# New places for two gatings' steps in expert 0, a last expert of 384 + 256 rows, and a second network in six tiles of three blocks

## The chip, the cores and the metric

The kernel runs on one core of a Trainium2 chip. The time is that of one execution on the device in microseconds (us), and less is better. The core's engines each work through a queue of their own: TensorE (PE, matmuls), VectorE (DVE), ScalarE (ACT), GpSimd (POOL, which also issues the indirect DMAs) and SyncE (SP, which issues most plain DMAs). A wait in a queue holds up everything behind it in that queue.

## The reference

Attention over windows of 64 positions, a mixture of eight experts with the two best for each token, and a dense second network. In short:

```
scores = q @ k.T / 8, masked to 0 <= i - j < 64;  x = softmax(scores) @ v      # 4 x 8 heads x 576 x 64
x = heads put side by side                                                     # 2304 tokens x 512
noisy = x @ w_gate + log1p(exp(x @ w_noise)) * noise                           # 8 experts
top2 = the two best experts of each token, with softmax weights
x = sum over the two: weight * (relu(x @ w1[e]) @ w2[e])                        # 512 -> 1024 -> 512
h = x @ w_in;  out = (h * clip(h + 3, 0, 6) / 6) @ w_out                       # 512 -> 2048 -> 512
```

All data are float32. The tokens are 18 blocks of 128.

## The kernel before, in words

Every product of the two networks is made from a high and a low part of each operand with three matmuls (high x high, high x low, low x high). A half is called `xh`/`xl` for tokens, `hh`/`hl` for the hidden layer, and `h..`/`l..` with two more letters for a weight.

**Attention** runs first, about 137 us. PE's order is written by hand; the order on DVE, ACT and POOL is made by a scheduler. Its last step for a group of heads, `normalise`, writes `xbuf` on DVE and so frees the PSUM tile `pv`.

**Gating** (`gate_batch`) works in four batches of 4, 5, 4 and 5 blocks. For each it makes the noisy logits (`logits`, `logits_back`, `s1` to `s2`), takes the two best (`s3`, `s3b`, which ends in the mask `mk`), counts the places on PE (`s4`), and derives a token's position (`s5`). `place` then builds for each block and choice two matrices on DVE, `pa` and `pbt`, whose product on PE adds token numbers into `px`; `total` adds this to `iacc`. After the last batch `iacc` becomes `idx`, the table by which `gather` fetches tokens from `x_rows`. Of the third batch only the start, and of the fourth nothing, is done during attention. The rest is hung into expert 0's first sub-stage by two lists of numbers, `when_late` (third) and `when` (fourth): number i below 32 is the place after the matmuls of step d = i % 4 of hidden block f = i // 4, and above that a place in the second layer. From expert 0 on, the order of all queues is the order of the program.

**Experts.** An expert handles up to 640 rows (5 blocks, m = 0 to 4) in two sub-stages: expert 0 in 256 + 384 rows (`SUBS`), the others in 320 + 320. A sub-stage (`expert_sub`) first makes the hidden layer, eight blocks f of 12 matmuls, each followed by `hh` on ACT and `hl` on DVE; then, for each m, 24 matmuls of the second layer, a copy `y` and its store to `y_rows`. The PSUM tiles of f are `ph` (three buffers), and every fourth one is `ph4` (one buffer), so f = 3 and f = 7 share it. Other work is hung into a sub-stage by `put(function, key)`, with keys ("f", f, 0 or 1), ("d", f, d), ("m", m, 0 to 3) and ("s", m, f).

**The second network** takes the blocks in tiles, 2, 3, 3, 3, 3, 2 and 2 blocks (`TILES`). A tile has two halves; each makes eight hidden blocks of 12 matmuls over the whole tile, then 24 matmuls per block. Its input is made by `fetch(t, i)` (8 indirect DMAs on POOL per block i of tile t, four pieces for each of a token's two experts, into `xg`), `combine` (ACT scales, DVE adds) and `tokens` (DVE transposes into `xt`, ACT makes `xh`, DVE `xl`). A fetch of token block n reads the rows of the first min(5, n + 1) blocks m of all experts, so block 0 needs m = 0 of expert 7 stored:

```
tt = BASES[t] + i
left = ybuf[0:E * 128 * min(CAP, tt + 1)]
```

Tile 0's two blocks are fetched, combined and turned during expert 7's second sub-stage; later tiles' during the tile before.

Of the kernel before, what the change touches and what calls it, by code (L numbers as in the profile page):

```python
# [32 lines left out]

HOLD = SUBS[0][1] * 128
# [11 lines left out]
def attention_moe_kernel(ctx, tc, q, k, v, w_gate, w_noise, noise, w1, w2, w_in, w_out, out):  # L46
# [282 lines left out]

    def gate_batch(ts, bank):  # L330
# [4 lines left out]
        def tmp(nm, shape=(E,), dt=F32):  # L335
            T[nm] = gp.tile([128, 5, *shape], dt, name=nm)[:, :n]
            return T[nm]
# [87 lines left out]

        def place(i, j):
            def run():
                t = t0 + i
                a = gp.tile([128, 128], F16, name="pa", bufs=4)
                bt = gp.tile([128, E * NT], F16, name="pbt", bufs=4)  # L430
                dve.tensor_scalar(a, iota128, T["qf"][:, i, j:j + 1], None, op0=OP.is_equal)
                dve.tensor_scalar(bt, iotab, T["cf"][:, i, j:j + 1], tokid[:, t:t + 1],
                                   op0=OP.is_equal, op1=OP.mult)
                PL[t, j] = (a, bt)
# [6 lines left out]
            return run, mm  # L441
# [24 lines left out]

        def runs(i):
            for run, mm in pl[2 * i:2 * i + 2]:
                run()

        def mms(i):
            for run, mm in pl[2 * i:2 * i + 2]:
                mm()
# [6 lines left out]
        if t0 + n == NT:  # L480
            chain = firsts + [logits, logits_back, s1, s1b, s2, s3, s3b, s4, s5]
            return (chain + [lambda i=i: runs(i) for i in range(n)] + [lambda i=i: mms(i) for i in range(n)] +
                    [total, weigh, piece_rows])
# [174 lines left out]
    fill, late, coming = [], [], []  # L658
# [9 lines left out]
    with tc.manual_schedule(engines={mybir.EngineType.PE}):  # L668
# [10 lines left out]
        for g in range(NG + 2):  # L679
            n, j = divmod(g, 3)  # L680
            for past in ((g - 3, g - 2) if g > 2 and g % 2 else ()):
# [3 lines left out]
                if p == HP - 1 and jj == 2 and b < B - 1:  # L685
                    t = gate_batch(DONE[b], lambda: gps.tile([128, 512], F32, name="g"))
                    if b == B - 2:
                        cut = [f for _, f in t].index(None) + 5
                        t, late = t[:cut], [f for _, f in t[cut:] if f]
# [190 lines left out]
    def expert_sub(e, s, at):  # L880

        m0, m1 = SUBS[s]


        if e == 0:
# [4 lines left out]
        if e == 0 or s == 0:  # L890
            HH[:] = [[ep.tile([128, 384], F32R, name=f"{nm}{f}") for f in range(8)] for nm in ("hh", "hl")]
# [52 lines left out]
    TILES = (2, 3, 3, 3, 3, 2, 2)  # L944
# [29 lines left out]
    for e in range(E):  # L974
# [7 lines left out]
        if e == 0:  # L982
            t = gate_batch(DONE[B - 1], lambda: eps.tile([128, 512], F32, name="py", bufs=2))
            t += [lambda m=m: gather(0, m) for m in range(A1, M)] + [lambda m=m: build(0, m) for m in range(A1, M)]
# [4 lines left out]
            assert len(when) == len(t) and len(when_late) == len(late)  # L989
            for i, f in list(zip(when_late, late)) + list(zip(when, t)):  # L990
                put(f, *(("d", i // 4, i % 4) if i < 32 else ("s", (i - 32) // 8, (i - 32) % 8)))
# [14 lines left out]
        if 0 < e < 5:  # L1006
            for f in range(8):
                put(lambda: next(table, None), "f", f, 1)
        expert_sub(e, 0, at)
# [31 lines left out]
        else:  # L1041
# [120 lines left out]
    for t, ni in enumerate(TILES):  # L1162
# [10 lines left out]
        if t + 1 < len(TILES):  # L1173
# [11 lines left out]
            if 0 < t < len(TILES) - 2:  # L1185
                put(lambda: fetch(t + 2, 0), 1, 1, 3)
# [7 lines left out]
        for half in range(2):  # L1194
# [18 lines left out]
            for i in range(ni):  # L1213
# [51 lines left out]
```

## Time and profile before

| | |
|---|---|
| median of 3 runs | 1007.03 us (1004.6 to 1007.49) |
| the profiled execution | 1009.37 us, of which its span 1007.6 |
| busy share of the span | PE 98%, DVE 57%, ACT 46%, POOL 32% |
| mean granted clock of PE | 0.991 |
| chain that ended last | PE 80%, DVE 9%, DMA 5%, ACT 3% of the span |

The profile is of one execution. Times in it count from the start of its span; what lies outside the span (1.8 us) is not in it. The chain follows the last instruction back, each time to what released it or to what stood ahead of it on its engine.

### The profile page before, as it was taken

The numbers are of one execution on the slowest core, as the hardware profiler recorded it, in microseconds if no ns is written. First come the engines' busy times: TensorE is split into PE (matmuls) and PEld (weight loads), VectorE is DVE, ScalarE is ACT, GpSimd is POOL, SyncE is SP. The second block draws the span as 40 slices with busy tenths as digits, with TensorE's granted clock in tenths as the row PEclk, the third lists the DMA queues.
The fourth block names the chain that finished last, engine by engine and source line by source line (L and its number), as shares of the span: only waits on it lengthen the run. The fifth ranks groups of instructions, "written<-read, shape, count | busy, mean of one in ns | idle before, by whom it ended". The sixth has DMA issues, their size and how long they took to land.

```text
span 1007.6 us, 17479 instructions
## 1 busy us (share of the span) xinstructions
PE 983.8 (98%) x6392; PEld 893.7 (89%) x6392; DVE 573.9 (57%) x1550; ACT 467.8 (46%) x1032; POOL 324.7 (32%) x351
## 2 busy tenths in 40 slices
PE   8989898999999999999999999999999999999998
PEld 7979886999897999999998988989988998899997
DVE  6687975556777776666667656444333433344322
ACT  6867651444544454444454546434333433334333
POOL 2122202732535334242431276732343234410000
PEclk9999998999999999999999999999999999999999
DMA  9897441546656666656666454200111002000000
GB/s 168 169 221 190 119 147 50 165 139 201 214 163 197 192 184 193 186 186 209 215 195 196 151 191 133 70 23 19 58 32 46 24 26 63 27 27 22 11 11 23
DMA packets 116395, 122.43 MB, mean 122 GB/s; under 512 B 69840, under 2 KB 78288, under 8 KB 116304
## 3 DMA queue, kind: packets, MB, share of 16 engines
q1 hardware_dynamic: 96144, 86.17, 31.0%
q0 software_dynamic: 9488, 19.94, 7.1%
q10 hardware_dynamic: 10672, 15.15, 4.1%
q8 instruction: 51, 0.84, 0.3%
q14 instruction: 40, 0.33, 0.1%
HBM read 92.91 MB, written 28.31 MB: 120 GB/s over the span
## 4 chain that ended last, share of the span: by engine, by line
PE 80%; DVE 9%; DMA 5%; ACT 3%; issue 2%; POOL 0%; ACTq 0%; DVEq 0%; SPq 0%
PE ph L1204 6%; PE ph L1202 6%; PE ph L1203 6%; PE ph L903 6%; PE ph L904 6%; PE ph L905 6%; PE py L1225 5%; PE py L1224 5%; PE py L1223 5%; PE py L923 4%; PE py L924 4%; PE py L925 4%; PE s L242 3%; PE pv L295 2%; PE tr L1225 1%
## 5 line engine op out<-in xcount | busy, mean ns | idle before, releaser
L522 POOL DMA_INDIRECT xg<-x_rows,idx x140 | 145.1, 1037 | 221.2 <-DVE xt L533 169.8
L959 POOL DMA_INDIRECT xg<-y_rows,rows x144 | 144.3, 1002 | 222.4 <-DVE xg L967 74.5
L1207 DVE SCALAR_TENSOR_TENSOR g<-g,ph 128x384 f32<-128x384 f32 (+1 forms) x112 | 55.7, 497 | 158.8 <-ACT g L1206 154.5
L1206 ACT ACTIVATE g<-ph,three 128x384 f32<-128x384 f32 (+1 forms) x112 | 60.0, 536 | 100.7 <-PE ph L1204 97.7
L911 DVE SCALAR_TENSOR_TENSOR hl<-ph,hh 128x320 fp32r<-128x320 f32 (+2 forms) x128 | 61.0, 487 | 74.1 <-ACT hh L910 74.1
L1212 DVE TENSOR_TENSOR hl<-g,hh 128x384 fp32r<-128x384 f32 (+1 forms) x112 | 56.2, 502 | 58.9 <-ACT hh L1210 56.1
L910 ACT ACTIVATE hh<-ph 128x320 fp32r<-128x320 f32 (+2 forms) x128 | 54.6, 436 | 65.2 <-PE ph L905 61.2
L1210 ACT CAST hh<-g 128x384 fp32r<-128x384 f32 (+1 forms) x112 | 52.4, 467 | 63.8 <-DVE g L1207 63.8
L527 ACT CAST xh<-xt 128x512 fp32r<-128x512 f32 (+1 forms) x60 | 33.6, 570 | 81.9 <-DVE xt L533 81.2
L528 DVE TENSOR_TENSOR xl<-xt,xh 128x512 fp32r<-128x512 f32 (+1 forms) x60 | 37.2, 630 | 39.7 <-ACT xh L527 39.7
L242 PE MATMUL s<-kt,qbd 128*128 128x128 f32 x288 | 43.7, 293 | 0.2 <-ACT kt L227 0.2
L242 PEld LDWEIGHTS s<-kt,qbd 128*128 128x128 f32 x288 | 40.2, 207 | 0.6 <-ACT kt L227 0.5
L157 POOL TENSOR_SCALAR vt<-vt 64x520 f32<-64x520 f32 (+1 forms) x32 | 19.3, 604 | 57.0 <-DMA vt<-in_v_dram 53.2
L533 DVE STREAM_TRANSPOSE xt<-xg 128x512 f32<-128x512 f32 x53 | 37.4, 706 | 0.4
L762 DVE SCALAR_TENSOR_TENSOR na<-mag,raw 128x256 f32<-128x256 f32 x64 | 26.9, 420 | 12.7 <-DMA w_out<-na 5.1
L759 ACT ACTIVATE mag<-raw 128x256 f32<-128x256 f32 x64 | 27.6, 431 | 12.6 <-DVE na L768 12.6
L257 ACT ACTIVATE pb<-sm,mx 128x128 f32<-128x128 f32 x90 | 30.0, 397 | 5.8 <-DVE mx L250 5.7
L768 DVE CUSTOM_DVE_ANT_0 na<-mag,nr 128x512 uint16<-128x512 uint16 x64 | 27.3, 426 | 9.5 <-DVE mag L767 0.5
L931 ACT COPY y<-py 128x512 f32<-128x512 f32 x33 | 19.3, 584 | 27.1 <-PE py L925 14.1
L270 ACT COPY ptb<-pt 128x384 f32<-128x384 f32 x48 | 23.1, 480 | 12.7 <-PE pt L265 10.7
L767 DVE SCALAR_TENSOR_TENSOR mag<-na,mag 128x256 int32<-128x256 int32 x64 | 27.2, 425 | 2.2
L295 PE MATMUL pv<-vt,ptb 128*64 128x65 f32 x640 | 26.1, 226 | 1.8 <-DVE xbuf L314 1.8
(520 smaller groups left out, 3201.7 us busy)
## 6 DMA issues: line engine op xcount, KB each, us to landing
wraw<-in_moe_w_dram SPq DMA_DIRECT2D x60, 512.0 KB, 4.6
y_rows<-y ACTq DMA_DIRECT2D x40, 256.0 KB, 3.4
raw<-in_moe_w_in_dram SPq DMA_DIRECT2D x32, 256.0 KB, 3.8
raw<-in_moe_w_out_dram SPq DMA_DIRECT2D x32, 256.0 KB, 3.0
rq<-in_q_dram SPq DMA_DIRECT2D x32, 144.0 KB, 3.7
rk<-in_k_dram SPq DMA_DIRECT2D x32, 144.0 KB, 2.9
x_rows<-xbuf SPq DMA_DIRECT2D x18, 256.0 KB
out_dram<-y ACTq DMA_DIRECT2D x17, 256.0 KB, 2.2
```

Of the source, the lines that this page charges most:

```text
L242: pe.matmul(s[:, i, :], l, KT[n][:, k0:k0 + 128], start=(g in LIGHT), stop=(g in LIGHT or i == 2))
L522: pool.indirect_dma_start(out=t[:, i], out_offset=None, in_=pieces(xrows), in_offset=bass.IndirectOffsetOnAxis(ap=idx4[:, i, e, m:m + 1], ...
L903: pe.matmul(p, wh[:, fs], xh[:, d, :n], start=(d == 0), stop=False)
L904: pe.matmul(p, wh[:, fs], xl[:, d, :n], start=False, stop=False)
L905: pe.matmul(p, wl[:, fs], xh[:, d, :n], start=False, stop=(d == 3))
L911: dve.scalar_tensor_tensor(hl[f][:, cs], p, 0.0, hh[f].bitcast(F32)[:, cs], op0=OP.max, op1=OP.subtract)
L959: pool.indirect_dma_start(out=g[:, r], out_offset=None, in_=pieces(left), in_offset=bass.IndirectOffsetOnAxis(ap=rows4[:, r, tt, j:j + 1], ...
L1202: pe.matmul(p, wh[:, c], xh[:, d, :n], start=(d == 0), stop=False)
L1203: pe.matmul(p, wh[:, c], xl[:, d, :n], start=False, stop=False)
L1204: pe.matmul(p, wl[:, c], xh[:, d, :n], start=False, stop=(d == 3))
L1206: act.activation(g, p, AF.Relu, bias=three)
L1225: pe.matmul(py[i], gl[f][:, ms], wh[:, ws], start=False, stop=(f == NF - 1))
```

## The change

It has three parts.

1. In expert 0 the rest of the third batch (now from `logits_back` on) and the fourth batch are hung at new places by a table, `steps`, with the same numbers i as before. On DVE some of the two batches' steps are interleaved, one instruction of each in turn (`weave`); for that, `place` is cut in its two instructions. `pa` and `pbt` have eight buffers instead of four, and `gw`, `qf` and `cf` two instead of one.
2. Expert 7 is split 384 + 256 (`LAST`). The fetches of tile 0's three blocks begin in its first sub-stage, and two of the three combinations stand in the hidden layer of its second one.
3. The second network has six tiles of three blocks.

```diff
-            when = [0, 1, 3, 5, 7, 10, 12, 12, 13, 14, 16, 18, 28, 28, 30, 31, 31, 32, 33,
-                    36, 37, 38, 39, 40, 40, 41, 44, 40, 40, 40, 45, 46, 47]
-            when_late = [2, 3, 14, 14, 24, 24, 25, 26, 27, 30]
+            steps = {0: [a_back, turns[0], a_s1, turns[1]],
...
+                     10: [lambda: weave(a_5(), b_2())],
+                     12: [b_s3],
+                     16: [lambda: weave(b_3b(), a_parts(0))],
+                     20: [lambda: weave(a_parts(1))],
+                     23: [b_s4],
+                     24: [lambda: a_mms(0)],
+                     26: [lambda: a_mms(1), lambda: weave(b_5(), a_parts(2) + a_parts(3))],
+                     28: [lambda: weave(b_parts(0))],
+                     33: [lambda: a_mms(2), lambda: a_mms(3), lambda: weave(b_parts(1)), a_total],
+                     34: [lambda: b_mms(0), lambda: weave(b_parts(2))],
...
+                     38: [lambda: b_mms(4), b_total] + [lambda m=m: gather(0, m) for m in range(A1, M)],
...
+    def weave(*lists):
+        for fs in itertools.zip_longest(*lists):
+            for f in fs:
+                if f:
+                    f()
...
-                a = gp.tile([128, 128], F16, name="pa", bufs=4)
-                bt = gp.tile([128, E * NT], F16, name="pbt", bufs=4)
+                PL[t0 + i, j] = (gp.tile([128, 128], F16, name="pa", bufs=8),
+                                 gp.tile([128, E * NT], F16, name="pbt", bufs=8))
...
+LAST = ((0, 3), (3, CAP))
...
+        if e + 1 == E:
+            put(lambda: fetch(0, 0), "m", 1, 2)
+            put(lambda: fetch(0, 1), "m", 2, 2)
         expert_sub(e, 0, at)
...
-            for i in range(2):
-                put(lambda i=i: fetch(0, i), "f", 3 * i, 0)
-                put(lambda i=i: combine(0, i), "m", A1 + i, i)
-                put(lambda i=i: tokens(0, i), "m", A1 + i, 1 + i)
+            for i, (c, k) in enumerate(((("f", 0, 0), ("f", 1, 0)), (("f", 3, 0), ("f", 4, 0)),
+                                        (("m", 3, 1), ("m", 3, 2)))):
+                put(lambda i=i: combine(0, i), *c)
+                put(lambda i=i: tokens(0, i), *k)
+            put(lambda: fetch(0, 2), "f", 2, 0)
+            put(lambda: fetch(1, 0), "m", 4, 2)
...
-            put(lambda: fetch(1, 0), "m", A1 + 2, 0)
...
-    TILES = (2, 3, 3, 3, 3, 2, 2)
+    TILES = (3,) * 6
...
-            if 0 < t < len(TILES) - 2:
+            if t < len(TILES) - 2:
                 put(lambda: fetch(t + 2, 0), 1, 1, 3)
```

What this does to DVE's queue is shown at three places, each before and after. A row is line, operation, output and inputs, and size; a number behind a name tells tiles of one name apart.

First, DVE in attention, among the placements of a gating batch (about 72 us). Before:

```order
L310 RECIPROCAL rs_1354<-rs_1354 128x4
L250 ISA sm_1387,mx_1386<-s_1382,far_135 128x128
L250 ISA mx_1386 128x1
L250 ISA sm_1387,mx_1386<-s_1382,far_135 128x128
L250 ISA mx_1386 128x1
L250 ISA sm_1387,mx_1386<-s_1382,far_135 128x128
L250 ISA mx_1386 128x1
L431 TENSOR_SCALAR pa_1442<-iota128_127,qf_1285 128x128
L432 TENSOR_SCALAR pbt_1443<-iotab_129,cf_1286,tokid_131 128x144
L431 TENSOR_SCALAR pa_1446<-iota128_127,qf_1285 128x128
L432 TENSOR_SCALAR pbt_1447<-iotab_129,cf_1286,tokid_131 128x144
L314 TENSOR_TENSOR xbuf_191<-pv_1211,rs_1354 128x8x32
```

After:

```order
L445 TENSOR_SCALAR pa_1504<-iota128_127,qf_1283 128x128
L448 TENSOR_SCALAR pbt_1505<-iotab_129,cf_1284,tokid_131 128x144
L312 RECIPROCAL rs_1354<-rs_1354 128x4
L252 ISA sm_1387,mx_1386<-s_1382,far_135 128x128
L252 ISA mx_1386 128x1
L252 ISA sm_1387,mx_1386<-s_1382,far_135 128x128
L252 ISA mx_1386 128x1
L252 ISA sm_1387,mx_1386<-s_1382,far_135 128x128
L252 ISA mx_1386 128x1
L248 TENSOR_REDUCE mx_1425<-s_1420 128x3
L311 TENSOR_SCALAR rs_1459<-pv_1322 128x6
L316 TENSOR_TENSOR xbuf_191<-pv_1211,rs_1354 128x8x32
```

The placements that stood between `sm` and `xbuf` are now ahead of `rs`, with two pairs more (of the four moved the last shows here), and an `mx` and an `rs` have come ahead of the `xbuf`, the row behind these.

Second, DVE in expert 0 around hidden blocks f = 3 to f = 5, where the fourth batch's mask `mk` and the third batch's first placements stand. Before:

```order
L392 TENSOR_TENSOR oh_2860<-iota8_92,ti_2843 128x80
L394 TENSOR_TENSOR mk_2861<-oh_2860 128x40
L911 SCALAR_TENSOR_TENSOR hl4_2650<-ph_2838,hh4_2642 128x256
L911 SCALAR_TENSOR_TENSOR hl5_2651<-ph_2869,hh5_2643 128x256
L431 TENSOR_SCALAR pa_2888<-iota128_127,qf_2819 128x128
L432 TENSOR_SCALAR pbt_2889<-iotab_129,cf_2820,tokid_131 128x144
L431 TENSOR_SCALAR pa_2892<-iota128_127,qf_2819 128x128
L432 TENSOR_SCALAR pbt_2893<-iotab_129,cf_2820,tokid_131 128x144
```

After:

```order
L396 MAX tm_2827<-gd_2804 128x8 x5
L398 MAX_INDEX ti_2828<-tm_2827,gd_2804 128x8 x5
L929 SCALAR_TENSOR_TENSOR hl3_2632<-ph_2823,hh3_2624 128x256
L403 TENSOR_TENSOR oh_2854<-iota8_92,ti_2828 128x80
L445 TENSOR_SCALAR pa_2857<-iota128_127,qf_2802 128x128
L405 TENSOR_TENSOR mk_2855<-oh_2854 128x40
L448 TENSOR_SCALAR pbt_2858<-iotab_129,cf_2803,tokid_131 128x144
L445 TENSOR_SCALAR pa_2862<-iota128_127,qf_2802 128x128
L448 TENSOR_SCALAR pbt_2863<-iotab_129,cf_2803,tokid_131 128x144
L929 SCALAR_TENSOR_TENSOR hl4_2633<-ph_2850,hh4_2625 128x256
```

The first two pairs of the third batch stood behind `mk` and two `hl`; now they are woven with `mk`, ahead of those `hl`.

Third, DVE in expert 7's second sub-stage, around hidden block f = 3 (`ph4`). Before:

```order
L911 SCALAR_TENSOR_TENSOR hl2_7263<-ph_7587,hh2_7255 128x320
L595 TENSOR_TENSOR lyb_7585<-wraw_7525,hyb_7584 128x1024
L911 SCALAR_TENSOR_TENSOR hl3_7264<-ph4_7603,hh3_7256 128x320
L911 SCALAR_TENSOR_TENSOR hl4_7265<-ph_7633,hh4_7257 128x320
L595 TENSOR_TENSOR lzb_7631<-wraw_7582,hzb_7630 128x1024
L911 SCALAR_TENSOR_TENSOR hl5_7266<-ph_7649,hh5_7258 128x320
L911 SCALAR_TENSOR_TENSOR hl6_7267<-ph_7664,hh6_7259 128x320
L911 SCALAR_TENSOR_TENSOR hl7_7268<-ph4_7684,hh7_7260 128x320
```

After:

```order
L929 SCALAR_TENSOR_TENSOR hl2_7597<-ph_7653,hh2_7589 128x256
L613 TENSOR_TENSOR lyb_7651<-wraw_7533,hyb_7650 128x1024
L985 SCALAR_TENSOR_TENSOR xg_7560<-xg_7565,gates4_110,xg_7560 128x128 x4
L929 SCALAR_TENSOR_TENSOR hl3_7598<-ph4_7679,hh3_7590 128x256
L548 STREAM_TRANSPOSE xt_7714<-xg_7560 128x4x4x32
L543 TENSOR_TENSOR xl0_7634<-xt_7714,xh0_7633 128x4x128
L929 SCALAR_TENSOR_TENSOR hl4_7599<-ph_7707,hh4_7591 128x256
L613 TENSOR_TENSOR lzb_7705<-wraw_7648,hzb_7704 128x1024
L929 SCALAR_TENSOR_TENSOR hl5_7600<-ph_7727,hh5_7592 128x256
```

The four additions of a combination (`xg`, x4), here those of block 1, now stand ahead of `hl3`, and the turning of that block ahead of `hl4`; before, all eight `hl` came first.

## Rows read from the trace of the kernel before

**Rows 1.** Page, first lines: busy us (share of span) xinstructions
```profile
PE 983.8 (98%) x6392; PEld 893.7 (89%) x6392; DVE 573.9 (57%) x1550; ACT 467.8 (46%) x1032; POOL 324.7 (32%) x351
```

**Rows 2.** Windows, second network: length; busy PE, PEld, DVE, ACT, POOL; clock; DMA; GB/s
```profile
602.30:648.70 46.40, 45.58 (x290) 40.96 (x289) 26.28 (x55) 24.73 (x54) 32.29 (x31) 1.00 0.37 111
648.70:714.70 66.00, 66.00 (x337) 60.35 (x336) 25.09 (x50) 24.73 (x50) 26.84 (x29) 1.00 0.14 40
912.90:957.70 44.80, 44.80 (x289) 41.05 (x288) 18.43 (x44) 18.92 (x44) 0.00 (x0) 1.00 0.03 13
```

**Rows 3.** Windows of expert 7's first and second sub-stage
```profile
546.90:571.90 25.00, 25.00 (x146) 23.09 (x145) 14.96 (x31) 12.07 (x24) 0.00 (x0) 1.00 0.48 153
571.90:602.30 30.40, 30.40 (x169) 27.59 (x168) 18.55 (x30) 15.15 (x28) 21.76 (x21) 1.00 0.61 198
```

**Rows 4.** Timeline, PE, expert 0: start, us; in brackets idle before, releaser
```profile
153.50 0.67 PE L440 MATMUL g<-pbt,pa 128*128 128x144 f16 x2 [1.62 <-DVE pbt L432]
...
171.56 0.66 PE L542 MATMUL tr<-ident,xg 128*128 128x128 f32 x4 [0.60 <-DMA xg<-x_rows,idx]
```

**Rows 5.** Windows around low and full granted clock (the column behind POOL)
```profile
74.70:78.10 3.40, 3.40 (x27) 3.27 (x22) 2.90 (x13) 2.33 (x6) 1.37 (x3) 0.50 0.89 272
153.20:160.00 6.80, 6.30 (x47) 5.73 (x48) 5.70 (x33) 0.59 (x2) 0.00 (x0) 0.50 0.01 2
309.40:314.00 4.60, 3.47 (x14) 2.29 (x13) 3.88 (x9) 2.34 (x4) 3.34 (x3) 1.00 0.45 142
```

**Rows 6.** Timeline of DVE in expert 0
```profile
152.19 0.20 DVE L394 TENSOR_TENSOR mk<-oh 128x40 f16<-128x40 f32 x1
...
167.66 0.23 DVE L452 CAST idx<-iacc 128x144 int32<-128x144 f32 x1
```

**Rows 7.** Timeline of POOL in expert 0
```profile
168.17 0.96 POOL L516 DMA_INDIRECT xg<-x_rows,idx  x1 [38.54 <-DVE gw L463]
```

**Rows 8.** Timeline of DVE in attention
```profile
72.30 0.96 DVE L431 TENSOR_SCALAR pa<-iota,qf 128x128 f16<-128x128 f16 x1
73.17 0.31 DVE L432 TENSOR_SCALAR pbt<-iotab,cf,tokid 128x144 f16<-128x144 f16 x1
...
73.56 0.31 DVE L432 TENSOR_SCALAR pbt<-iotab,cf,tokid 128x144 f16<-128x144 f16 x1
73.78 0.41 DVE L314 TENSOR_TENSOR xbuf<-pv,rs 128x256 f32<-128x256 f32 x1
...
112.29 0.41 DVE L314 TENSOR_TENSOR xbuf<-pv,rs 128x256 f32<-128x256 f32 x1
```

**Rows 9.** Timeline of PE in attention
```profile
74.25 0.78 PE L295 MATMUL pv<-vt,ptb 128*64 128x65 f32 x16 [1.78 <-DVE xbuf L314]
...
114.64 0.57 PE L295 MATMUL pv<-vt,ptb 128*64 128x65 f32 x12
```

**Rows 10.** Timeline of PE, first layer-two matmul of tile 5
```profile
924.41 0.40 PE L1223 MATMUL py<-hwa,hh 128*128 128x512 f32 x1
```

**Rows 11.** Timeline of POOL in expert 7
```profile
572.60 0.99 POOL L959 DMA_INDIRECT xg<-y_rows,rows  x1 [34.62 <-DVE mag L767]
573.89 0.94 POOL L959 DMA_INDIRECT xg<-y_rows,rows  x1 [0.30 <-issue]
...
592.23 1.81 POOL L959 DMA_INDIRECT xg<-y_rows,rows  x1 [0.30 <-issue]
```

**Rows 12.** Page's DMA issues: engine op xcount, KB each, median us to landing
```profile
y_rows<-y ACTq DMA_DIRECT2D x40, 256.0 KB, 3.4
```

**Rows 13.** Tile xg from 566 to 600 us
```profile
DMA to landing us min/median/max: 2.4/2.7/4.8
```

**Rows 14.** Timeline of DVE in expert 7
```profile
591.99 1.23 DVE L595 TENSOR_TENSOR lwa<-wraw,hwa 128x1024 fp32r<-128x1024 f32 x1 [0.26 <-ACT hwa L589]
...
597.32 0.35 DVE L967 SCALAR_TENSOR_TENSOR xg<-xg,gates 128x128 f32<-128x128 f32 x1 [1.97 <-DMA xg<-y_rows,rows]
...
599.11 0.69 DVE L528 TENSOR_TENSOR xl<-xt,xh 128x512 fp32r<-128x512 f32 x1 [0.69 <-ACT xh L527]
```

More of the change, by code (lines that the diff above doesn't have):

```diff
@@ L335, in tmp @@
         def tmp(nm, shape=(E,), dt=F32):
[L336 removed]
+            T[nm] = gp.tile([128, 5, *shape], dt, name=nm, **({"bufs": 2} if nm in ("gw", "qf", "cf") else {}))[:, :n]
             return T[nm]
@@ new lines, in s5, with first, second @@
+        def s5():
+            weave(parts5())
+        def place(i, j):
+            def first():
+                PL[t0 + i, j] = (gp.tile([128, 128], F16, name="pa", bufs=8),
+                                 gp.tile([128, E * NT], F16, name="pbt", bufs=8))
+                dve.tensor_scalar(PL[t0 + i, j][0], iota128, T["qf"][:, i, j:j + 1], None, op0=OP.is_equal)
+            def second():
+                dve.tensor_scalar(PL[t0 + i, j][1], iotab, T["cf"][:, i, j:j + 1], tokid[:, t0 + i:t0 + i + 1],
+                                  op0=OP.is_equal, op1=OP.mult)
@@ L440, in mm @@
                 pe.matmul(T["px"], a, bt, start=(i == 0 and j == 0), stop=(i == n - 1 and j == 1))
-            return run, mm
+            return first, second, mm
         pl = [place(i, j) for i in range(n) for j in range(2)]
@@ L465, in weigh, with parts @@
             dve.tensor_tensor(g[:, :, 1], w[:, :, 1], g[:, :, 0], op=OP.mult)
+        def parts(i):
+            return [f for p in pl[2 * i:2 * i + 2] for f in p[:2]]
         def runs(i):
-            for run, mm in pl[2 * i:2 * i + 2]:
-                run()
+            weave(parts(i))
         def mms(i):
-            for run, mm in pl[2 * i:2 * i + 2]:
-                mm()
+            for p in pl[2 * i:2 * i + 2]:
+                p[2]()
         def last():
@@ L479, in gate_batch @@
         lg[0] = bank()
[L480 to L483, printed above, removed]
+        if t0 >= DONE[B - 2][0]:
+            return firsts, logits, logits_back, s1, s1b, s2, parts2, s3, parts3b, s4, parts5, parts, mms, total, weigh, piece_rows
         chain = [("tr", f) for f in firsts] + [("col", logits)]
@@ L553, in build @@
             turn_rows(XG[e, m], *columns(e, s), 128 * (m - SUBS[s][0]))
+        elif e + 1 == E:
+            s = int(m >= LAST[0][1])
+            turn(XG[e, m], (*columns(e, s), 128 * (m - LAST[s][0])))
         elif m == 2:
@@ L657, in attention_moe_kernel @@
         pe.matmul(warm[:, 0:128], ones, ones, start=True, stop=True)
-    fill, late, coming = [], [], []
+    fill, coming, third = [], [], None
     def bg(*kinds, n=1):
@@ L687, in attention_moe_kernel @@
                     if b == B - 2:
-                        cut = [f for _, f in t].index(None) + 5
-                        t, late = t[:cut], [f for _, f in t[cut:] if f]
+                        third = t
+                        t = [("tr", f) for f in t[0]] + [("col", t[1])]
                     coming += t
@@ L990, in attention_moe_kernel @@
-            for i, f in list(zip(when_late, late)) + list(zip(when, t)):
-                put(f, *(("d", i // 4, i % 4) if i < 32 else ("s", (i - 32) // 8, (i - 32) % 8)))
+            fourth_of = gate_batch(DONE[B - 1], lambda: eps.tile([128, 512], F32, name="py", bufs=2))
+            a_back, a_s1, a_s1b, a_s2, _, a_s3, a_3b, a_s4, a_5, a_parts, a_mms, a_total, a_weigh = third[2:15]
+            (turns, b_logits, b_back, b_s1, b_s1b, _, b_2, b_s3, b_3b, b_s4, b_5, b_parts, b_mms, b_total, b_weigh,
+             b_rows) = fourth_of
@@ L992, in attention_moe_kernel @@
+            for m in range(A1, M):
+                steps[44 + m - A1] = [lambda m=m: build(0, m)]
+            for i, fs in steps.items():
+                for f in fs:
+                    put(f, *(("d", i // 4, i % 4) if i < 32 else ("s", (i - 32) // 8, (i - 32) % 8)))
         else:
```

78 lines of the change are left out of this document (43 added, 35 removed).

## The prediction

> **What bounds the kernel now.** I began with the page: the matrix engine (PE) is busy for 98% of the span [rows 1], so the time is the sum of what PE has to do and of the places where it stops or runs slowly. Then I read windows stage by stage. The second network is full: a tile of three blocks takes 66.0 us and is busy for 66.0, one of two blocks 44.8 for 44.8; only its first tile has slack, 45.58 busy in 46.4 [rows 2]. Expert 7 is full too, 25.0 and 30.4 us [rows 3]. So neither of these stages can gain except by doing less, and both can lose. Expert 0 is different: the row of PE has a wait of 1.62 us for a `pbt` at 153.50 and one of 0.60 us for a gathered block at 171.56 [rows 4], and after the first of them the granted clock is 0.50 (1.2 of 2.4 GHz) from 153.2 to 160.0 [rows 5]. The profiled execution took 1009.37 us (span 1007.6), 2.3 above the median 1007.03; I sum changes against the first and carry the sum to the median.
>
> **The second network in six tiles: -4.0 us.** Before: 46.4 + 4 x 66.0 + 2 x 44.8 = 400.0. After: 6 x 66.0 = 396.0. Of the 4.0, 2.4 is certain (three tiles of two blocks, 134.4, become two of three, 132.0: fewer matmuls carry the same columns); the other 1.6 is what the first tile loses against 44.8, in waits on the halves while it still prepares weights. Those steps stay in tile 0, but each f step there gives the other engines 384 columns' time instead of 256, so I count the whole. Bounds -2.4 and -4.0.
>
> **Expert 0: -4.0 us.** Third gating's first two `pa`/`pbt` pairs now stand ahead of two `hl` rows, beside the fourth's `mk` (second excerpt), so the 1.62 us go, and with them the half clock, whose 6.8 us at 0.50 [rows 5] cost 3.4: together 5.0. In the traces a wait of about a microsecond did not lower the clock: between 309.4 and 314.0 PE was busy for 3.47 of 4.60 us and the clock stayed at 1.00 [rows 5]. I give back 1.0: the fourth's `mk` was done at 152.39 [rows 6] and its reader, the counting matmuls, now stands a step earlier, which by my walk through the new DVE order with the old durations leaves a wait of about 0.4, and the first fourth placement waits about 0.6 for the third's sum `iacc`. The index `idx` was ready at 167.9 [rows 6] and the gathers left at 168.17 [rows 7]; both move with the stage, about 4 us earlier, so the 0.60 us wait for the first gathered block stays as it is. Bounds: -2.0 if a wait long enough for one half-clock stretch remains, -5.5 if nothing is given back and the gather is hidden too.
>
> **Attention: +3.1 us.** The diff does not touch it by intent, but with eight `pa`/`pbt` buffers the scheduler puts placements earlier on DVE (first excerpt). Around 72 us two more pairs, and an `mx` and an `rs`, stand ahead of the `xbuf` whose end at 74.19 frees the PSUM that PE waits for [rows 8]; PE already waits 1.78 us there [rows 9]. A pair costs 0.39 (`pbt` to `pbt`, 73.17 to 73.56), `mx` and `rs` about 0.6 by the starts behind them: 1.4. Around 112 us five pairs, an `mx` and two `qbd` copies move ahead of `xbuf`, which ended at 112.70 [rows 8]; PE took the buffer at 114.64 without a wait [rows 9], so 1.9 us are cover. My walk puts its end near 116.3: 1.7. Work moved forward is not done later, so DVE may give some back before PE asks again; against that a new wait of 1.7 us could buy a half-clock stretch like that from 74.7 to 78.1 [rows 5], 1.7 more. Bounds 0 and +6.
>
> **Expert 7 and the start of the second network: +9.8 us.** The split 384 + 256 costs nothing: a sub-stage has the matmuls of half a tile, 66.0/2 = 33.0 and 44.8/2 = 22.4, together 55.4 as before (25.0 + 30.4) [rows 2, 3]. The price is in what must arrive before tile 0. Before, two blocks of tokens, 16 indirect transfers; now three, 24; and two of the three combinations stand inside the second sub-stage. Let s be expert 7's start.
> - The transfers can begin when block m=0 is stored. One block of the second layer takes (22.4 - 11.5)/2 = 5.45 us, with 11.5 from 912.90 to 924.41 [rows 2, 10]. Before, m=0 ended at 571.9 - 5.45 = 566.45 and the first transfer was issued at 572.60 [rows 11], 6.15 later; the store alone lands 3.4 after its issue [rows 12], and with about 0.9 for the copy and the issue, an estimate, 4.3 is the floor. I take 5.5. Now m=0 ends at s + (33.0 - 2 x 5.45) = s + 22.1, and the first transfer is at s + 27.6.
> - Sixteen took 572.60 to 594.04, 1.34 each; undisturbed one takes 0.94 + 0.30 [rows 11]. The sixteenth starts at s + 27.6 + 15 x 1.34 = s + 47.7 and lands 2.7 later [rows 13]: s + 50.4.
> - DVE's queue (third excerpt) has the combination of block 1 (`xg`, x4) ahead of `hl3`. DVE stops there until that landing, and `hl3` holds the PSUM buffer `ph4` that f=7 writes next. With the last `xg` (0.35 [rows 14]) and an `hl` of about 0.4, f=7 can start at s + 51.2. PE is there at s + 33.0 + 7/8 x 11.5 = s + 43.1. It loses 8.1, and 1.7 more as the clock is then at 0.50 for a stretch like those in [rows 5].
> - Behind it the 24th transfer lands at s + 27.6 + 23 x 1.34 + 2.7 = s + 61.1, and from `xg` to `xl` it takes 597.32 to 599.80 [rows 14]: tile 0's data are ready at s + 63.6. PE, delayed, is there at s + 65.2, so this adds nothing; but it means that without the stall at f=7 the loss would still be 63.6 - 55.4 = 8.2. Before, tile 0's data were ready at 599.80 and it started at 602.32, 2.5 us of cover.
>
> Bounds: first transfer at 4.3, 1.24 a piece, landing 2.4, no clock loss: the sixteenth lands at s + 47.4 and f=7 waits 5.1, tile 0's data are there at s + 59.8: 4.4, so +5.1; with 6.15, landing 4.8 and the clock: +12.6.
> The long issue of 1.81 us [rows 11] lay beside the `lwa` at 591.99 [rows 14], a DVE subtraction of two SBUF operands, so 1.34 contains such collisions. The Trainium skill ("SBUF — State Buffer", Who interferes with whom) says that such a `tensor_tensor` takes only the shared read interface while writing descriptors needs the write one, marked as inferred, so it should not slow them. By that rule a piece takes 1.24 and the term is 8.3 instead of 9.8; the row speaks against it.
>
> **Sum:** -4.0 - 4.0 + 3.1 + 9.8 = +4.9. Profiled execution 1009.4 to 1014.3; median 1007.03 to **1011.9**.
>
> **Rivals.**
> 1. *Faster.* The queue stop is hidden: if the first combination is late but f=7's buffer is not (the sixteenth transfer lands by s + 43), and tile 0's data by s + 55, the term is 0 and the sum -4.9 (1002.1), or -8 with attention at 0 (999). It decides at a transfer period of about 0.85 us; the shortest issues of a row alone take 1.24. Chance 0.08.
> 2. *No measurable change.* The transfers cost their lower bound of 5.1 and attention 0 to 3: sum -2.9 to +0.2, 1004 to 1007.5; the page's rule alone, 8.3, with attention at 0 gives 1007.3. Chance 0.2.
> 3. *Heavier.* Collisions stretch the 24 transfers and every new wait lowers the clock: 12.6 + 6 - 4 - 2.4 at most, about 1019. Chance 0.12.
> 4. *The gating places do not do what they say:* the wait only moves to another `pbt` and expert 0 gains 0 to 1: 1015. Chance 0.1.
> The forecast, 1008.5 to 1015 with all terms as above, has 0.5.
>
> The range 1005 to 1018 leaves out most of rival 1 and the end of 3. A change of under 0.3% (3.0 us, the spread of the three runs shown) cannot be told from none. Faster by more needs rival 1: 0.08. Within it: rival 2 and the low end of the forecast: 0.22. Slower: 0.70.
>
> **What would show it.** In the new profile: PE in expert 0 without the wait for `pbt` and with clock 1.00 between 150 and 165, first layer's end 4 us earlier; POOL's row of 24 transfers without a pause in expert 7; a PE wait of some 8 us for `hl` in the second sub-stage, and none at tile 0; PE waits for `xbuf` near 75 and 116 us. If the transfers run under 1 us each, or start before s + 25, the largest term falls and the kernel is faster; if tile 0 waits as well, it is slower than said.

## The result, and the profile after

Six executions of the changed kernel took 1014.07 us in the median (1012.80 to 1017.87), six of the kernel before 1006.02 (1004.60 to 1007.49); the ratio is 1.0073 with a 95% interval of 1.0056 to 1.0090, so +7.3 us (5.6 to 9.1). Forecast were +4.9 and 1011.9, slower with 0.70. The direction is as forecast and the median lies in the range of 1005 to 1018; the size is 2.4 us over the sum.

The profiled execution of the changed kernel took 1012.89 us. Its page:

```profile
span 1011.0 us, 16998 instructions
...
PE 978.1 (97%) x6200; PEld 888.1 (88%) x6200; DVE 566.0 (56%) x1517; ACT 459.2 (45%) x999; POOL 323.7 (32%) x351
```

PE is busy for 5.7 us less than before [rows 1], and the span is 3.4 us longer: its idle time grew by 9.1 us. The windows by stage, with the columns of [rows 2]:

```profile
137.70:154.80 17.10, 17.10 (x200) 16.55 (x200) 12.84 (x85) 6.11 (x18) 0.00 (x0) 1.00 0.45 147
541.40:574.40 33.00, 33.00 (x169) 30.18 (x168) 17.42 (x33) 14.15 (x26) 4.03 (x4) 1.00 0.52 165
574.40:608.10 33.70, 25.77 (x146) 22.87 (x145) 17.08 (x32) 13.88 (x30) 21.48 (x21) 0.90 0.38 120
592.00:596.00 4.00, 2.87 (x13) 2.88 (x14) 3.32 (x8) 2.28 (x5) 3.17 (x3) 0.50 0.20 54
596.00:599.40 3.40, 3.40 (x11) 2.67 (x10) 2.66 (x5) 0.48 (x2) 2.91 (x2) 0.62 0.55 172
608.10:674.10 66.00, 64.94 (x330) 58.83 (x329) 31.83 (x57) 29.80 (x56) 37.06 (x38) 1.00 0.32 98
674.10:740.20 66.10, 66.10 (x338) 60.41 (x337) 25.08 (x50) 24.72 (x50) 23.18 (x25) 1.00 0.13 36
```

Expert 7's first sub-stage is full and takes 33.0 us, as half a tile does. The second takes 33.7 instead of 22.4, is busy for 25.8 of them, and has the granted clock at 0.50 after the longest wait. Tile 0 now takes 1.06 us of waits, tile 1 none. These are PE's waits, first in expert 7, then in tile 0:

```profile
582.36 0.38 PE L921 MATMUL ph<-xh,hwa 128*128 128x256 f32 x1 [2.03 <-DVE hl L929]
...
584.70 0.39 PE L921 MATMUL ph<-xh,hwa 128*128 128x256 f32 x1 [0.65 <-DVE hl L929]
...
593.13 0.58 PE L921 MATMUL ph<-xh,hwa 128*128 128x256 f32 x1 [5.26 <-DVE hl L929]
```

```profile
630.43 0.50 PE L1271 MATMUL py<-hza,hh 128*128 128x512 f32 x1 [0.73 <-ACT hh L1258]
...
631.49 0.50 PE L1273 MATMUL py<-hza,hl 128*128 128x512 f32 x1 [0.33 <-DVE hl L1260]
```

2.03 + 0.65 + 5.26 = 7.94 us, all for an `hl`. The first two stand at f = 4 and f = 5, which need the `hl` of f = 0 and f = 1; on DVE these stand behind the combination and the turning of block 0. The third stands at f = 7, which needs the `hl` of f = 3, behind block 1's combination. POOL's fetches and DVE's queue show why they are late. On POOL the first, second, sixteenth, 22nd and last of the 24 transfers:

```profile
569.46 1.77 POOL L977 DMA_INDIRECT xg<-y_rows,rows  x1 [37.09 <-DVE na L786]
571.53 0.94 POOL L977 DMA_INDIRECT xg<-y_rows,rows  x1 [0.30 <-issue]
...
589.61 0.94 POOL L977 DMA_INDIRECT xg<-y_rows,rows  x1 [0.30 <-issue]
...
597.66 1.82 POOL L977 DMA_INDIRECT xg<-y_rows,rows  x1 [0.30 <-issue]
...
601.03 0.94 POOL L977 DMA_INDIRECT xg<-y_rows,rows  x1 [0.30 <-issue]
```

And on DVE:

```profile
569.19 1.22 DVE L613 TENSOR_TENSOR lwb<-wraw,hwb 128x1024 fp32r<-128x1024 f32 x1
...
591.86 0.88 DVE L985 SCALAR_TENSOR_TENSOR xg<-xg,gates 128x128 f32<-128x128 f32 x3 [1.14 <-DMA xg<-y_rows,rows]
592.65 0.42 DVE L929 SCALAR_TENSOR_TENSOR hl<-ph,hh 128x256 fp32r<-128x256 f32 x1
...
597.44 1.22 DVE L613 TENSOR_TENSOR lva<-wraw,hva 128x1024 fp32r<-128x1024 f32 x1
...
605.51 0.69 DVE L543 TENSOR_TENSOR xl<-xt,xh 128x512 fp32r<-128x512 f32 x1 [0.69 <-ACT xh L542]
```

The first transfer goes out 28.1 us after the expert's start (541.40), the sixteenth at 48.2. DVE's last three additions of block 1 (`xg`) end at 592.7, `hl` follows at once, and PE goes on at 593.13. The 1.14 us that DVE waited at 591.86 were for the fourteenth transfer, which landed 4.9 us after its issue at 586.89. The last transfer is issued at 601.03, and tile 0's last `xl` is done at 606.2, before PE comes to tile 0 at 608.07.

In expert 0 the 1.62 us wait for `pbt` of [rows 4] and the half clock behind it [rows 5] are gone: the window from 137.7 to 154.8 is full at 1.00. One wait is left, for the third batch's sum, and the gathers leave at 163.38 instead of 168.17 [rows 7]:

```profile
158.67 0.29 PE L455 MATMUL g<-pbt,pa 128*128 128x144 f16 x2 [1.33 <-DVE iacc L465]
```

```profile
163.38 0.96 POOL L531 DMA_INDIRECT xg<-x_rows,idx  x1 [33.12 <-DVE gw L478]
```

From the first hidden block to expert 1, expert 0 takes 137.69 to 204.86, 67.17 us; before it took 137.26 to 209.70, 72.44. In attention, four waits of PE answer to [rows 9]:

```profile
74.12 0.69 PE L297 MATMUL pv<-vt,ptb 128*64 128x65 f32 x16 [2.87 <-DVE xbuf L316]
...
111.94 0.84 PE L267 MATMUL pt<-ident,pb 128*128 128x128 f32 x3 [0.70 <-ACT pb L259]
...
114.54 0.68 PE L297 MATMUL pv<-vt,ptb 128*64 128x65 f32 x15 [0.42 <-DVE xbuf L316]
...
129.17 0.66 PE L557 MATMUL tr<-ident,xg 128*128 128x128 f32 x4 [1.47 <-DMA xg<-x_rows,idx]
```

The wait for `xbuf` grew from 1.78 to 2.87. Near 112 us, where PE did not wait before, it now waits 0.70 for `pb` (ACT, whose input is an `mx` from DVE) and 0.42 for `xbuf`, and 1.47 for a gather that took 0.93.

So the two profiles give +0.4 in attention, -5.3 in expert 0, +11.3 in expert 7 (541.40 to 608.07 against 546.91 to 602.32), -2.3 in the second network and -0.7 elsewhere: +3.4, the difference of the spans. The medians differ by 8.05. The profiled execution of before was a long one of its kind (1009.37 against 1006.02); where its length lay was the first thing to find out.

### The profile page after: what moved, and what is told of

Same layout as the page of the kernel before. It is cut to its first block, busy times and chain, and to the rows that moved or that the text cites. A ratio compares the mean times of both kernels' runs of the same rounds, so it can differ in the third digit from the quotient of the medians.

```text
span 1011.0 us, 16998 instructions
## 1 busy us (share of the span) xinstructions
PE 978.1 (97%) x6200; PEld 888.1 (88%) x6200; DVE 566.0 (56%) x1517; ACT 459.2 (45%) x999; POOL 323.7 (32%) x351
## 4 chain that ended last, share of the span: by engine, by line
PE 77%; DVE 9%; DMA 6%; ACT 3%; issue 3%; POOL 1%; SPq 0%; ACTq 0%; DVEq 0%; POOLq 0%
PE ph L1252 6%; PE ph L1250 6%; PE ph L1251 6%; PE ph L921 6%; PE ph L922 6%; PE ph L923 5%; PE py L941 4%; PE py L943 4%; PE py L942 4%; PE py L1273 4%; PE py L1272 4%; PE py L1271 4%; PE tr L1273 2%; PE tr L1272 2%; PE tr L1271 2%
## 5 line engine op out<-in xcount | busy, mean ns | idle before, releaser
L1255 DVE SCALAR_TENSOR_TENSOR g<-g,ph 128x384 f32<-128x384 f32 x96 | 53.2, 554 | 163.1 <-ACT g L1254 162.9
L1254 ACT ACTIVATE g<-ph,three 128x384 f32<-128x384 f32 x96 | 55.7, 581 | 110.9 <-PE ph L1252 110.3
L1260 DVE TENSOR_TENSOR hl<-g,hh 128x384 fp32r<-128x384 f32 x96 | 53.6, 558 | 53.9 <-ACT hh L1258 53.9
L1258 ACT CAST hh<-g 128x384 fp32r<-128x384 f32 x96 | 49.3, 514 | 60.0 <-DVE g L1255 60.0
L921 PE MATMUL ph<-xh,hwa 128*128 128x320 f32 (+2 forms) x80 | 25.7, 321 | 7.9 <-DVE hl L929 7.9
L985 DVE SCALAR_TENSOR_TENSOR xg<-xg,gates 128x128 f32<-128x128 f32 x72 | 21.1, 347 | 18.7 <-ACT xg L984 11.4
```

What stands on the lines that cost most here:

```text
L921: pe.matmul(p, wh[:, fs], xh[:, d, :n], start=(d == 0), stop=False)
```

## The experiments

Times are medians beside the kernel before on the same chip; the ratio has a 95% interval, and "+x us" is the ratio's.

**One part at a time.** `x1_gating` is the changed kernel with the last expert, its fetches and the tiles as before. `x2_buffers` is:

```diff
-                a = gp.tile([128, 128], F16, name="pa", bufs=4)
-                bt = gp.tile([128, E * NT], F16, name="pbt", bufs=4)
+                a = gp.tile([128, 128], F16, name="pa", bufs=8)
+                bt = gp.tile([128, E * NT], F16, name="pbt", bufs=8)
```

`x3_tiles` is the kernel before with `LAST`, its fetches and combinations, and `TILES = (3,) * 6`. `x5_split` has `LAST` alone, with the weight steps of that sub-stage at the changed kernel's places and the two combinations at

```diff
-                put(lambda i=i: combine(0, i), "m", A1 + i, i)
-                put(lambda i=i: tokens(0, i), "m", A1 + i, 1 + i)
+                put(lambda i=i: combine(0, i), "m", 3 + i, 0)
+                put(lambda i=i: tokens(0, i), "m", 3 + i, 1)
```

> The kernel before with the first part of the change alone: new places for the last two gatings' steps in expert 0, eight pa/pbt buffers; old last expert, old tiles. Two theories of where the 8.05 us between the medians come from, of which the two profiles show only 3.4. A (the profiles are typical in attention): attention +0.4, expert 0 -5.3, so 1006.0 - 4.9 = about 1001. B (the new order of attention costs several us in most executions and the one profile of before was a long one): attention +3 to +5, expert 0 -5.3, so 1004 to 1006.

> The kernel before with eight instead of four buffers for pa and pbt and nothing else: the scheduler then gives attention the order that it has in the changed kernel, and expert 0 keeps its old places. A: +0.4 us, no difference that can be told. B: +3 to +5 us, 1009 to 1011. In the profile, by either, a longer PE wait for xbuf near 74 us (2.9 instead of 1.8).

> The kernel before with the second and third part alone: last expert 384 + 256, three blocks fetched ahead of tile 0, six tiles of three blocks; old gating places and old attention order. Queue-and-transfer theory: expert 7 +11.3 us, second network -2.3, so 1006.0 + 9.0 = about 1015 by A as by B. If it is under 1011, the stall in expert 7 hangs on something from the first part.

> The kernel before with the last expert in 384 + 256 rows and nothing else: two-block tile 0, 16 transfers in the second sub-stage as before, the two combinations in the second layer (its first and second block there), seven tiles. Theory: the split itself costs nothing (33.0 + 22.4 = 25.0 + 30.4), 1006 +/- 1; the shorter second sub-stage (22.4 instead of 30.4 us) leaves less time for the 16 transfers: first at s + 33.5, sixteenth landing at s + 33.5 + 20.1 + 2.7 = s + 56.3 plus 2.5 against s + 55.4, so up to +3.4 at tile 0. Rival (the split is the culprit): +8 or more.

Measured, with before at 1006.48: `x1_gating` 1004.70, ratio 0.9987 (0.9975 to 0.9999), -1.3 us; `x2_buffers` 1011.34, 1.0054 (1.0037 to 1.0071), +5.4; `x3_tiles` 1013.58, 1.0089 (1.0063 to 1.0114), +9.0; `x5_split` 1009.29, 1.0030 (1.0016 to 1.0043), +3.0.

Theory B holds: eight buffers for two small matrices cost 3.7 to 7.1 us, though PE, DVE, ACT and POOL have as many instructions as before. The waits of PE with buffers alone, in the rows of attention:

```profile
73.66 0.69 PE L295 MATMUL pv<-vt,ptb 128*64 128x65 f32 x16 [2.62 <-DVE xbuf L314]
...
111.78 0.85 PE L265 MATMUL pt<-ident,pb 128*128 128x128 f32 x3 [0.77 <-ACT pb L257]
...
129.12 0.66 PE L542 MATMUL tr<-ident,xg 128*128 128x128 f32 x4 [1.57 <-DMA xg<-x_rows,idx]
```

They are those of the changed kernel, and so is the order: DVE's 491 instructions of attention stand in one order in before, `x3_tiles` and `y7_own` (below), and in another one in after, `x1_gating` and `x2_buffers`. In the four profiles with the old order (before, `x3_tiles`, `x5_split`, `y7_own` below) expert 0's first hidden block starts at 137.26, 133.14, 138.11 and 136.11 us, mean 136.2; in the six with the new (after, `x1_gating`, `x2_buffers`, and `y0_changed`, `y4_queue`, `y6_other` below) at 137.69, 138.44, 137.64, 141.62, 140.95 and 141.97, mean 139.7 (on the slower chip below it was 133.21 with the old, 136.71 and 137.67 with the new). So attention scatters by 5 us from one execution to the next in the same order, and a pair of profiles can show 0.4 where the runs give 5.4. Low clock is part of the scatter (about 10 us of attention at 0.50 in before, 20 in `x5_split`), but before and `x3_tiles`, both with 10, are 4.1 us apart; that was not traced further.

`x3_tiles` has the stall of the changed kernel in a kernel without the first part, its largest wait the same within 0.01 us:

```profile
593.75 0.58 PE L907 MATMUL ph<-xh,hwa 128*128 128x256 f32 x1 [5.27 <-DVE hl L915]
```

The split alone was not free. Its hidden layer and its second layer ran at 11.5 and 10.9 us without a wait, as the sum had it, but tile 0 waited:

```profile
604.35 0.39 PE L1206 MATMUL ph<-xh,hsa 128*128 128x256 f32 x1 [1.91 <-ACT xh L528]
```

The sixteen transfers were the smaller part of it. They went out from 575.08, 28.2 us after the expert's start and not the 33.5 that was expected (POOL runs ahead of PE as soon as m = 0 is stored), and the sixteenth at 595.98:

```profile
575.08 1.78 POOL L963 DMA_INDIRECT xg<-y_rows,rows  x1 [37.14 <-DVE na L772]
...
595.98 0.94 POOL L963 DMA_INDIRECT xg<-y_rows,rows  x1 [0.30 <-issue]
```

ACT waited 0.40 us for the landing, and on DVE the turning of the second block stood behind a weight half (`lxa`) for 1.1 us, in a sub-stage of 22.4 instead of 30.4 us:

```profile
600.22 1.28 ACT L970 ACTIVATE xg<-xg,gates 128x128 f32<-128x128 f32 x4 [0.40 <-DMA xg<-y_rows,rows]
...
601.80 1.22 DVE L599 TENSOR_TENSOR lxa<-wraw,hxa 128x1024 fp32r<-128x1024 f32 x1
```

So `xh` ended 2 us late, and about 3 us behind the wait ran at a clock of 0.50 (13.5 instead of 11.5 us for tile 0's first hidden layer). That these 3 us belong to the places of the steps, and not to the split as such, is read from the rows; other places were not tried.

**The transfers.** `x4_queue` moves the combinations, and with them the third block's fetch, behind the hidden layer; `x6_other` takes away the wait for the store of m = 0 and hangs two fetches one block earlier. In `x6_other` tile 0's tokens come from rows of w1.

```diff
-            for i, (c, k) in enumerate(((("f", 0, 0), ("f", 1, 0)), (("f", 3, 0), ("f", 4, 0)),
-                                        (("m", 3, 1), ("m", 3, 2)))):
-            put(lambda: fetch(0, 2), "f", 2, 0)
+            for i, (c, k) in enumerate(((("f", 7, 1), ("f", 7, 1)), (("m", 3, 0), ("m", 3, 1)),
+                                        (("m", 4, 0), ("m", 4, 2)))):
+            put(lambda: fetch(0, 2), "f", 7, 1)
```

```diff
+        if t == 0:
+            left = ap_of(w1, 0, [[DM, E * CAP * 128], [1, DM]])
-            put(lambda: fetch(0, 0), "m", 1, 2)
-            put(lambda: fetch(0, 1), "m", 2, 2)
+            put(lambda: fetch(0, 0), "m", 0, 2)
+            put(lambda: fetch(0, 1), "m", 1, 2)
```

`x7_own` is `x1_gating` with matrices of their own for the third and fourth batch, so that the first two keep four buffers and attention its old order:

```diff
-                PL[t0 + i, j] = (gp.tile([128, 128], F16, name="pa", bufs=8),
-                                 gp.tile([128, E * NT], F16, name="pbt", bufs=8))
+                x, b = ("", 4) if t0 < DONE[B - 2][0] else ("x", 8)
+                PL[t0 + i, j] = (gp.tile([128, 128], F16, name="pa" + x, bufs=b),
+                                 gp.tile([128, E * NT], F16, name="pbt" + x, bufs=b))
```

> The changed kernel with the combinations of tile 0's blocks moved behind the hidden layer of expert 7's second sub-stage (block 0 after f = 7, blocks 1 and 2 in the second layer; the third block's fetch moves behind the first turning). Queue-and-transfer theory with two floors: PE no longer stops at f = 7, but the 24th transfer still goes out near s + 59.6 and tile 0's tokens are ready near s + 65, against s + 55.4, so the 8 to 9 us wait reappears at tile 0 and the time stays within 2 us of the changed kernel's 1014. Rival (DVE's queue order alone is the cause): the wait is gone, 1004 to 1006.

> The changed kernel, but tile 0's three blocks are fetched from rows of the input w1 instead of from the experts' results, which takes away the wait for the store of m = 0; the 24 transfers are issued half a second-layer block into expert 7's first second-layer block. Tile 0's tokens are then other numbers than the reference's. Queue-and-transfer theory: first transfer near s + 19, sixteenth landed near s + 42 (PE wants f = 7 at s + 43), 24th landed and turned near s + 55: the stall of 11.3 us falls to 0 to 2, time 1014 - 10 = 1003 to 1006. Rival (24 transfers beside the weights cost this much wherever they start): 1010 or more.

> The first part alone (new places in expert 0, old last expert and tiles), with pa and pbt buffers of its own for the third and fourth batch (eight) and the old four for the first two, so that attention keeps its old order. If attention's new order costs the 5 us of the run with buffers alone: 1006.5 - 6.5 = about 1000. If the places in expert 0 gain only as much as the first run showed and the order is not the cause: 1004 to 1005.

These three ran on a chip where the kernel before took 1047.18 us. Measured there: `x4_queue` 1050.52, 1.0035 (1.0009 to 1.0062); `x6_other` 1034.13, 0.9855 (0.9825 to 0.9885); `x7_own` 1041.17, 0.9950 (0.9928 to 0.9972). PE stops on that chip where it did not in the ten profiles from other chips, and for nothing that the trace names, here in expert 0's second sub-stage of `x4_queue`:

```profile
180.90 0.34 PE L923 MATMUL ph<-xh,lwa 128*128 128x384 f32 x1 [1.79 <-issue]
...
183.73 0.48 PE L922 MATMUL ph<-xl,hxa 128*128 128x384 f32 x1 [1.62 <-issue]
```

So they were timed again, beside the changed kernel itself:

> The changed kernel itself, on the same chip as the three runs behind it. The runs of the second job came from a chip on which the kernel before takes 1047 us, and PE there has idle stretches of 1 to 2 us that no semaphore ends, in expert 0's second sub-stage and around the fetches of expert 7; so the three kernels are timed once more beside the changed one. On a chip that gives the kernel before 1006: 1014 +/- 2, e0's first phase to expert 1 about 67 us, expert 7 66.7 us.

> Combinations moved behind the hidden layer, as before. Two-floors theory: within 2 us of the changed kernel, expert 7's hidden layer back at 11.5 us and a wait of 8 to 9 us at tile 0. Rival (DVE's queue order alone): 8 us under the changed kernel.

> Tile 0 fetched from rows of w1, no wait for the store of m = 0, as before; tile 0's tokens are other numbers than the reference's. Queue-and-transfer theory: 9 to 11 us under the changed kernel. Rival (the transfers cost as much wherever they start): within 3 us of it.

> First part alone with attention's old order, as before: 6 us under the kernel before (1000 on a chip that gives that 1006), as attention's new order cost 5 in the run with buffers alone. If only 2 us under, the new order was not the cause.

Measured, with before at 1006.65: `y0_changed` 1014.59, ratio 1.0074 (1.0056 to 1.0092); `y4_queue` 1014.47, 1.0076 (1.0057 to 1.0094); `y6_other` 1006.42, 1.0001 (0.9991 to 1.0011); `y7_own` 1001.72, 0.9952 (0.9934 to 0.9971).

`y4_queue`: two floors. The hidden layer of the second sub-stage is full again, 11.5 us, and the wait stands at tile 0 instead, with a low clock behind it; the median is 0.1 us from the changed kernel's:

```profile
610.22 0.69 PE L1250 MATMUL ph<-xh,hsa 128*128 128x384 f32 x1 [8.77 <-ACT xh L542]
```

```profile
578.90:590.40 11.50, 11.50 (x98) 11.50 (x97) 5.02 (x8) 5.30 (x11) 8.76 (x10) 1.00 0.55 176
610.20:630.10 19.90, 19.84 (x97) 19.44 (x98) 11.20 (x18) 10.13 (x18) 14.29 (x14) 0.84 0.53 166
```

`y6_other`: 8.2 us under the changed kernel, a little short of the 9 to 11 expected. The second sub-stage is full at 22.6 us, so the stall is gone with the wait for m = 0. But tile 0's hidden layer takes 21.4 instead of 16.7:

```profile
579.90:602.50 22.60, 22.60 (x145) 20.40 (x144) 14.07 (x30) 12.22 (x29) 9.70 (x8) 1.00 0.39 129
602.50:623.90 21.40, 18.85 (x97) 18.27 (x97) 12.05 (x17) 11.00 (x19) 13.14 (x13) 0.92 0.52 161
```

There PE waits for `g`, whose first instruction on ACT stands behind the half of a `w_out` weight (`hza`) that waited for its load:

```profile
613.91 0.44 PE L1252 MATMUL ph<-xh,hsa 128*128 128x384 f32 x1 [2.27 <-DVE g L1257]
```

```profile
610.75 1.05 ACT L607 CAST hza<-wraw 128x1024 fp32r<-128x1024 f32 x1 [1.52 <-DMA wraw<-w_out]
...
612.69 0.58 ACT L1256 ACTIVATE g<-ph,three 128x384 f32<-128x384 f32 x1 [0.40 <-ACT y L949]
```

In the changed kernel tile 0 starts 5.6 us later (608.07 against 602.51) and its hidden layer is full, so the stall seems to hide the same loads. The first transfer of `y6_other` went out before expert 7 began, not at s + 19: with nothing to wait for, POOL runs ahead.

`y7_own`: -4.8 us (-6.6 to -2.9), the same share as on the other chip, a little short of the 6 expected, and faster than both kernels. Against the -1.3 of `x1_gating`, which has the same places in expert 0, the old order of attention is worth 3.5 us; against before, the new one costs 5.4 in `x2_buffers`. Attention's row near 112 us is without a wait, and the wait for `iacc` in expert 0 is that of the changed kernel:

```profile
73.28 1.13 PE L297 MATMUL pv<-vt,ptb 128*64 128x65 f32 x16 [2.35 <-DVE xbuf L316]
...
127.59 0.66 PE L558 MATMUL tr<-ident,xg 128*128 128x128 f32 x4 [1.06 <-DMA xg<-x_rows,idx]
...
156.97 0.29 PE L456 MATMUL g<-pbtx,pax 128*128 128x144 f16 x2 [1.24 <-DVE iacc L466]
```

## Why the prediction was right in direction and short in size

- **What bounds the kernel.** Right: of the stages that were full expert 7 lost, the second network gained by fewer matmuls alone, and expert 0 gained.
- **Expert 0, -4.0.** The mechanism was right: the wait for `pbt` and the half clock went, a wait for `iacc` came (1.33 where 0.6 was put), none for `mk`. Measured -5.3 in the profiles and -4.8 (-6.6 to -2.9) with attention's order kept; its first sub-stage took 38.75, 38.89, 38.03 and 36.61 us in the profiles with the old places and 33.2 to 33.5 in six with the new. Too small, because the waits at the gathered blocks, which I left as they were, went nearly all: for the blocks from 1.05 to 0.19 us, for the `xh` behind them from 0.68 to none. The half clock of 3.4 is not there in every execution: the 36.61 are of `x5_split`, which has the same wait for `pbt` and no low clock behind it (last section).
- **Attention, +3.1.** The place and the cause were right: with buffers alone +5.4 (3.7 to 7.1). The wait for `xbuf` near 74 us grew by 1.1 in the profile (1.4 forecast). Near 112 us the step was off: PE waits mostly for `pb`, behind an `mx` that is late on DVE, 0.53 to 2.17 us in the six profiles with the new order, and only 0.42 for `xbuf` (0.73 at most), where 1.7 were forecast. What I did not see is the gather of expert 0's first block, half a microsecond later. In the profile these three make 2.75; the rest of the 5.4 is not traced to a row, and the low clock after longer waits may be in it, which is not shown.
- **The split.** Right that the matmuls cost nothing (33.0 and 11.5 + 10.9 in the window of the stage); wrong that it can be had alone for nothing: the shorter second sub-stage crowds the steps behind, +3.0 (1.6 to 4.3) in `x5_split`. In the changed kernel it cannot be told from the stall.
- **Expert 7, +9.8.** The chain was right and its times near: first transfer at s + 28.1 (27.6), sixteenth at s + 48.2 (47.7), waits of 7.94 us (8.1), PE on at s + 51.7 (51.2), tile 0's tokens at s + 64.8 (63.6). Not forecast were the two waits of 2.68 us in all behind block 0's combination; they take from the wait at f = 7, whose end they do not move, and so leave the sum. Nor was the last landing that DVE stopped for the sixteenth's but the fourteenth's, late by 2 us; the sixteenth was in when the last addition began, near 592.4. The low clock was mis-sized: it lasted from 593.1 to about 598.5 us and cost 2.7, not 1.7; 0.7 more lie in the matmuls at the edges of the three waits, which the sum had at nothing, so the term is 11.3. That the loss would be much the same without the stop in DVE's queue was forecast at 8.2 and shown by `y4_queue`. The period was 1.37 a transfer (569.46 to 601.03, 23 steps), against 1.34.
- **The second network, -4.0.** It gained 2.3, about its lower bound: tile 0 kept its waits on the halves (0.73 + 0.33), which I had counted as gone.

The terms as measured alone, -4.8 + 5.4 + 9.0 (second and third part together), make +9.6 for +7.3 measured; the intervals of the three are 1.7 to 2.6 us to each side, so the difference is within them. The first part as a whole (`x1_gating`, -1.3) and the other two (+9.0) make +7.7. The forecast's +4.9 was short by 2.3 in attention, 1.5 in expert 7 and 1.7 in the second network, and long by about 1 in expert 0.

Of the rivals, the one with the transfers hidden would have needed a period of 0.85; none was seen under 1.24. By the rule that a subtraction on DVE doesn't slow the issue, the term would have been 8.3; the changed kernel's rows speak against it again: from the first issue to the sixteenth, 20.15 us, 1.4 us are what subtractions on DVE added to four issues (below).

## What to carry to other kernels

Before a stage is made shorter or its successor's first piece larger, lay the chain of what the first piece needs (the last store, the number of transfers times their period, the landing, the turning) against the time that the stage leaves: here 24 transfers at 1.37 us, the first at 28 us, did not fit in 55. A larger number of buffers is a change to a scheduled part even where no code of that part is touched: give a later user buffers of its own. A difference of a few us in a part whose length scatters by 5 us from one execution to the next is priced by repeated runs, not by two profiles.

## What the runs showed of the hardware

- An indirect DMA's issue on POOL took 0.94 us alone, and 1.77, 1.82 and up to 2.0 us beside a 128x1024 subtraction of two SBUF operands on DVE (569.46 beside `lwb` at 569.19, 597.66 beside `lva` at 597.44). In ten profiles the 40 to 43 issues that shared over half a microsecond with one took 1.28 to 1.36 us in the mean, the 199 to 206 that shared none 0.95 to 0.96. The Trainium skill ("SBUF — State Buffer", Who interferes with whom) infers that a `tensor_tensor` leaves descriptor writing alone. Here the issue of an indirect DMA as a whole, which also reads its row numbers (`rows`) from SBUF, is held up; whether it is the reading or the writing that waits, no run shows. The mean hides a plain rule, which the rows above bear: `lwb` ends at 570.41 and the issue beside it 0.82 us later, at 571.23; `lva` at 598.66 and the issue at 599.48. All 341 issues of the ten profiles that began at least 0.03 us after the start of such a subtraction, with over 0.2 us of it left, ended 0.81 to 0.82 us after its end. None of the 122 that began with DVE idle, 0.1 to 0.9 us ahead of one, took more than 0.96 us, and none of the 162 that began inside a DVE instruction with one operand in PSUM (`hl<-ph,hh`, `g<-g,ph`, `xl<-tr,xh`) more than 0.95. So what counts is which of the two begins first, and how much of the subtraction is left.
- A wait of 5.26 us was followed by the clock at 0.50 from its end at 593.1 to about 598.5 us. But a wait of 2.87 near 74 us in the changed kernel had the clock at 1.00 on either side in that execution, and in `y0_changed`, the same kernel, a wait of 2.90 there had 6.3 us at 0.50 behind it. The wait of 1.62 for `pbt` at 153 us before had 6.8 us at 0.50 [rows 5], the same wait in `x5_split` none. Whether a wait costs clock differs from one execution to the next; a term for it needs both ends. The two waits, of `y0_changed` and of `x5_split`, and the window behind each:

```profile
74.76 1.14 PE L297 MATMUL pv<-vt,ptb 128*64 128x65 f32 x16 [2.90 <-DVE xbuf L316]
154.36 0.61 PE L441 MATMUL g<-pbt,pa 128*128 128x144 f16 x2 [1.62 <-DVE pbt L433]
```

```profile
74.70:81.00 6.30, 6.24 (x45) 6.05 (x46) 2.85 (x10) 2.33 (x7) 2.96 (x4) 0.50 1.03 257
150.00:165.00 15.00, 12.45 (x95) 10.01 (x93) 12.94 (x76) 1.74 (x5) 0.00 (x0) 1.00 0.00 1
```

- One chip ran the same program 4% slower (1047 against 1006), with idle stretches on PE that no semaphore ended, most of them in the stages where POOL gathers. Those of 0.5 to 2.3 us make 13 to 15 us in each of its three profiles, whose spans are 27 to 35 us longer than those of the same kernels elsewhere, so they are not all of it. What holds PE there was not tried.
